# Products with the sines on GpSimd, and a sign moved to a later copy, in a two-branch sequence mixer

## The chip, the cores and the metric

The kernel runs on one core of one Trainium2 chip. The metric is the device time of one execution in microseconds (us), the median of three runs. A core has five engines that work side by side, each through its own queue in order: TensorE (PE, matmuls into PSUM; PEld is its weight load), VectorE (DVE), ScalarE (ACT), GpSimd (POOL) and SyncE (SP, which only issues DMAs here; ACT and POOL issue some too). They wait for each other by semaphores.

## The reference

Two branches read the same input of 2048 positions by 640 channels, and a gate by position mixes them:

```python
g = _sigmoid((x * gate_w).sum(-1, keepdims=True))
a = _A_ref(x, ...)      # long convolution by FFT with K, plus x * D_skip
b = _B_ref(x, ...)      # 2-D FFT, times a complex filter, inverse 2-D FFT
return g * a + (1 - g) * b
```

The convolution's kernel K is made from 128 complex modes for each of the 640 channels. This is the part that the change edits:

```python
dt = jnp.exp(log_dt)
A = -jnp.exp(log_A_real) + 1j * A_imag
C = (C_real + 1j * C_imag) * dt[:, None]
P = jnp.exp((A * dt[:, None])[:, :, None] * pos[None, None, :])
K = 2.0 * jnp.einsum("dn,dnl->dl", C, P).real
```

## The kernel before

**Phase P** turns the parameters into per-mode magnitudes and angles, `par`, in split high and low parts. **Phase A** transforms the input along the sequence: a first stage of small matmuls (`stage1`, L328), a copy out of PSUM, a second stage (`stage2`, L340), and the result goes to DRAM as `u_d`. The second half of the same function is the other branch: for each of nine groups of frequencies it loads `ue`, folds it (`fo`, `fg`), transposes it, transforms it along the channels (`p_d`), multiplies by the filter (`filt`, L528: `mm`, `zz`, `pm`), and transforms it back (`p_eo`, `p_i`). **Phase C** makes the first stage of K's transform, **phase D** the rest: the product of the two spectra, the inverse transform, the gates and the output.

**Phase B** makes K. It runs over 40 tiles of 16 channels each. K at position 64m + a is a product of two factors by mode: `y` for the 32 steps m and `x` for the 64 positions a, so that a matmul over the 128 modes (on the partitions) gives it. The positions a are counted from their middle, so that the two halves of 32 share the cosine and the sine of one angle: on the far half the angle has the other sign. One tile `t` has these steps:

- `mags` (L632): three matmuls `p_e` of 128x512 and three ACT exponentials give `e`, 16 channels by 96: 64 magnitudes for `x`, 32 for `y`. They run for five tiles (BT) in a row, so that ACT changes its table of functions twice for five tiles.
- `phases` (L643): two matmuls `p_p` give the angles in turns, ACT adds a large constant (L651) and DVE takes it away with the angle (L652), which leaves the reduced angle `q`, 1024 elements: the first 512 for `x`, the second for `y`.
- `trig` (L655): DVE clears the sign (`aq`, L662), and ACT makes four sines of 512 elements: the sines of `q` (sine) and of `aq` with a bias (cosine). For `y` they go to SBUF (`sc`, L665 and L666), for `x` to PSUM (`sx` L667, `cx` L668). `sx` and `cx` have one PSUM buffer each; `q`, `aq` and `sc` share five SBUF buffers.
- `prods` (L670): DVE multiplies the magnitudes by `sx` and `cx` (`x`, L675 to L677) and POOL by `sc` (`y`, L679 and L680).
- `kgen` (L682): 32 pairs of small matmuls of `y` and `x` accumulate `p_k` in PSUM, ACT copies two tiles at once to `kt` (L701), and every ten tiles go to DRAM as `k_d`.

`run` (L705) writes the order within phase B: in a burst of five tiles it takes `phases` and `trig` of tile t, then `prods` of t - 1, then a `kgen` some two tiles behind; between bursts come the five `mags`, with the `kgen` that are left. `merge` (L163) deals out the two streams, phase B against phases A and C, by the costs that each step yields (L228). Within that, a scheduler sets the final order of each engine's queue.

In phases C and D, `first` (L752) takes K's first transform: `stage1` with the table `e1` multiplies `kt`, and `S.copy` takes 512 columns at a time out of PSUM into `t1` (L336). What it copies has the 64 positions a of the real part on partitions 0 to 63, those of the imaginary part on 64 to 127, and in each the near half first.

## Time and profile before

| | |
|---|---|
| median of three runs | 609.23 us (608.76 to 611.23) |
| profiled execution | 608.74 us, of which the span of its instructions is 607.0 us |
| granted TensorE clock | 0.966 of full speed, mean |
| HBM | 60.91 MB read, 39.98 MB written, 166 GB/s over the span |

Three stages follow from the lines that run in them: up to 60 us the loads, phase P and the begin of phase A; from 60 to 430 us phase B beside the rest of phase A and the first of phase C; from 430 to 607 us phase D. The first sine of phase B stands at 72 us, its last product at 431 us.

A row of the groups of lines reads: line, engine, operation, what it writes <- what it reads, partitions x elements, count | busy us, mean ns of one | idle us of the engine before them, and what ended most of it. A row of waits reads: who, its line <- whom it waited for: us in total, times, longest. A row of the timeline: start us, duration us, engine, line, operation, operands.

### The profile page before, as it was taken

To read this page: it belongs to the slowest core of one execution; us is meant where nothing else is said; L and a number is where in the kernel's file an instruction comes from. 1 tells how busy PE (TensorE), PEld (TensorE's weight loads), DVE (VectorE), ACT (ScalarE), POOL (GpSimd) and SP (SyncE) were. 2 spreads that over 40 slices of the span, in tenths; PEclk is the share of its full clock that TensorE was granted. 3 is DMA by queue.
4 is the path that set the end of the run, shared out by engine and by line. 5 is a ranking of instruction groups with operands and counts; after the bars stand their busy time and mean duration, and the time that the engine had idled before them with its cause. 6 is when DMAs were issued, how large, how long until landed. Compare 5 with 4: busy or idle time off the path is not lost.

```text
span 607.0 us, 16654 instructions
## 1 busy us (share of the span) xinstructions
PE 535.8 (88%) x7084; PEld 405.6 (67%) x7084; DVE 500.2 (82%) x748; ACT 364.8 (60%) x659; POOL 267.0 (44%) x246
## 2 busy tenths in 40 slices
PE   9688979989968989989798999898989999999874
PEld 7576657766656657676566676565878877787631
DVE  5971597598899989999999899979399796987974
ACT  4556775576846876888589888799723332231210
POOL 4931252053525344454326335416254347547441
PEclk9899989989989996998899999999999999999998
DMA  8787204245612320332250233006685989889776
GB/s 341 293 288 268 79 5 151 69 154 181 239 43 67 97 87 13 108 118 109 67 151 12 75 97 110 24 28 200 224 346 184 356 273 299 291 271 310 225 231 239
DMA packets 48083, 101.98 MB, mean 168 GB/s; under 512 B 3316, under 2 KB 32776, under 8 KB 46248
## 3 DMA queue, kind: packets, MB, share of 16 engines
q1 hardware_dynamic: 24888, 67.74, 32.3%
q10 hardware_dynamic: 20080, 22.52, 11.9%
q0 software_dynamic: 3040, 10.65, 5.3%
q8 instruction: 56, 0.92, 0.6%
q14 instruction: 19, 0.16, 0.1%
HBM read 60.91 MB, written 39.98 MB: 166 GB/s over the span
## 4 chain that ended last, share of the span: by engine, by line
PE 51%; DVE 27%; ACT 9%; DMA 8%; issue 4%; POOL 1%; ACTq 0%; DVEq 0%; POOLq 0%; SPq 0%
PE p_eo L551 8%; PE p_s L348 8%; PE p_s L335 6%; PE p_e L638 5%; PE p_k L693 4%; PE p_i L814 4%; PE p_p L649 3%; DVE q L652 3%; PE p_d L518 2%; DVE t L801 2%; PE p_i L565 2%; PE p_t L502 2%; DVE ma L795 2%; PE p_c L893 2%; PE p_d L519 2%
## 5 line engine op out<-in xcount | busy, mean ns | idle before, releaser
L679 POOL TENSOR_TENSOR y<-e,sc 128x512 f32<-128x512 f32 x40 | 56.7, 1418 | 131.0 <-ACT sc L665 60.3
L348 PE MATMUL p_s<-t,w 128*64 128x160 f32 x1056 | 92.4, 314 | 10.2 <-ACT ut L382 5.1
L348 PEld LDWEIGHTS p_s<-t,w 128*64 128x64 f32 x1056 | 76.5, 139 | 21.4 <-ACT ut L382 6.0
L640 ACT ACTIVATE e<-p_e 128x512 f32<-128x512 f32 x120 | 68.6, 602 | 22.7 <-PE p_e L638 20.4
L551 PE MATMUL p_eo<-td,pmt 107*128 107x321 f32 x204 | 69.0, 459 | 3.9 <-ACT pmt L505 3.9
L693 PE MATMUL p_k<-x,y 128*32 128x64 f32 x2560 | 63.6, 229 | 9.8 <-DVE x L677 2.9
L693 PEld LDWEIGHTS p_k<-x,y 128*32 128x32 f32 x2560 | 46.1, 113 | 38.0 <-issue 29.4
L652 DVE SCALAR_TENSOR_TENSOR q<-q,p_p 128x512 f32<-128x512 f32 x80 | 53.4, 681 | 13.5 <-ACT q L651 11.8
L336 ACT COPY t<-p_s 128x512 f32<-128x512 f32 x40 | 24.6, 623 | 65.2 <-PE p_s L335 41.8
L638 PE MATMUL p_e<-rm,par 128*128 128x512 f32 x120 | 58.7, 519 | 3.4 <-ACT e L640 2.8
L680 POOL TENSOR_TENSOR y<-e,sc 128x512 f32<-128x512 f32 x40 | 54.5, 1362 | 6.5 <-ACT sc L666 6.5
L800 POOL TENSOR_TENSOR t<-ma 64x320 f32<-64x320 f32 x32 | 28.0, 875 | 61.4 <-DVE ma L795 51.8
L551 PEld LDWEIGHTS p_eo<-td,pmt 107*128 107x128 f32 x204 | 38.4, 198 | 19.6 <-ACT pmt L505 6.9
L677 DVE TENSOR_TENSOR x<-e,cx 128x1024 f32<-128x1024 f32 x40 | 48.6, 1214 | 2.2 <-ACT cx L668 2.2
L651 ACT ACTIVATE q<-p_p 128x512 f32<-128x512 f32 x80 | 46.5, 592 | 4.2 <-PE p_p L649 3.8
L649 PE MATMUL p_p<-rp,par 128*128 128x512 f32 x80 | 43.5, 548 | 4.5 <-DVE q L652 4.5
L814 PE MATMUL p_i<-t,w 128*64 128x160 f32 x528 | 42.7, 300 | 4.4 <-POOL t L801 3.4
L335 PE MATMUL p_s<-c,kt 128*64 128x128 f32 x640 | 43.0, 274 | 3.9 <-DVE mb L796 2.0
L335 PEld LDWEIGHTS p_s<-c,kt 128*64 128x64 f32 x640 | 38.0, 136 | 12.6 <-issue 7.7
L816 ACT COPY s<-p_i 128x640 f32<-128x640 f32 x32 | 21.8, 694 | 40.0 <-PE p_i L814 30.4
L335 PE MATMUL p_s<-c,u 128*64 128x128 f32 x640 | 41.5, 278 | 2.5 <-ACT ut L382 2.5
L795 DVE TENSOR_TENSOR ma<-p_s,us 128x640 f32<-128x640 f32 (+1 forms) x36 | 28.2, 784 | 18.8 <-PE p_s L348 11.5
(153 smaller groups left out, 1181.5 us busy)
## 6 DMA issues: line engine op xcount, KB each, us to landing
u_d<-ut SPq DMA_DIRECT2D x32, 320.0 KB, 2.6
us<-u_d ACTq DMA_DIRECT2D x16, 640.0 KB, 6.0
s_d<-s ACTq DMA_DIRECT2D x15, 640.0 KB, 8.3
t<-s_d SPq DMA_DIRECT2D x14, 640.0 KB, 5.9
ww<-in_w_l SPq DMA_DIRECT2D x8, 642.0 KB, 4.0
ue<-u_d SPq DMA_DIRECT2D x8, 640.0 KB, 4.4
k_d<-kt SPq DMA_DIRECT2D x4, 1280.0 KB, 7.6
kt<-k_d SPq DMA_DIRECT2D x8, 640.0 KB, 5.9
```

What stands on the lines that cost most here:

```text
L335: nc.tensor.matmul(p[64 * ri:64 * ri + 64, j, :], src(i + j), e1[ri], start=True, stop=True)
L348: ins = nc.tensor.matmul(p[64 * j:64 * j + 64, i, 160 * ri:160 * ri + 160], w2[:, x, 64 * ri:64 * ri + 64], t1[:, x // 2 if x < 32 else K0 ...
L551: P.matmul(p[:, :E], st.pmt[:DC, c, w, j, :], tv[:DC, w, c, :], start=c == 0, stop=c == 2)
L638: P.matmul(p[:, :], pars[t], rm[:, c:c + 512], start=True, stop=True)
L640: st.exp = S.activation(ef[:, c:c + 512], p[:, :], AF.Exp)
L649: P.matmul(p[:, :], pars[t], rp[:, c:c + 512], start=True, stop=True)
L652: V.scalar_tensor_tensor(out=qf[:, c:c + 512], in0=qf[:, c:c + 512], scalar=MAGIC, in1=p[:, :], op0=ALU.subtract, op1=ALU.subtract)
L677: V.tensor_tensor(out=x[:, 0].rearrange("p d (h j) -> p d h j", h=2), in0=e[:, :, 0:64].rearrange("p d (h j) -> p d h j", h=2), in1=cx.uns ...
L679: G.tensor_tensor(out=y[:, 1], in0=e[:, :, 64:96], in1=sc[:, 0], op=ALU.mult)
L680: G.tensor_tensor(out=y[:, 0], in0=e[:, :, 64:96], in1=sc[:, 1], op=ALU.mult)
L693: P.matmul(st.pb[32 * r:32 * r + 32, o, :], y[:, ri, 4 * qq + JR[r], :], x[:, ri, 4 * qq + JR[r], :], start=t % 2 + qq + 1 - ri == 0, stop ...
L814: T.mm = P.matmul(p[x:x + 64, i // 2, 160 * (i % 2):160 * (i % 2) + 160], T.w3[:, k0 + h + i, x:x + 64], t2[:, h + i, :], start=True, stop ...
```

## The change

ACT writes the sines over `q` and the `y` half of the cosines over `aq`, in SBUF; only `cx` stays in PSUM, with two buffers in place of one each for `cx` and `sx`. POOL makes the products with `sx`, both halves in one operation of 1024 elements with the sine broadcast over the two halves, between its two products of `y`. DVE makes the products with `cx`, one half plain and the far half times -1. Before, the far half's sine product carried the -1; now its cosine product does, so that the far half of `x` has the opposite sign as a whole. That sign goes through `kgen`, `k_d` and `stage1`, and is taken away where `first` copies out of PSUM: `near` scales each partition by +1 or -1 from a new column of the constant table. The skip term of `kgen` is untouched.

```diff
+        np.tile(np.repeat([1.0, -1.0], 32), 2)[:, None], np.full((128, 1), HALF_PI)], 1)
...
+        T.sa = take(1)
...
-    pt = ctx.enter_context(tc.tile_pool(name="b_pt", reuse_waits="tile", bufs=1, space=PSUM))
+    pt = ctx.enter_context(tc.tile_pool(name="b_pt", reuse_waits="tile", bufs=2, space=PSUM))
...
     def trig(t, r):
-        aq = wt.tile([128, 2, 16, 32], F32, tag="w", name="aq")
-        sc = r.sc = wt.tile([128, 2, 16, 32], F32, tag="w", name="sc")
-        sx, cx = r.sx, r.cx = [pt.tile([128, 16, 32], F32, tag=n, name=n) for n in ("sx", "cx")]
+        aq = r.aq = wt.tile([128, 2, 16, 32], F32, tag="w", name="aq")
+        cx = r.cx = pt.tile([128, 16, 32], F32, tag="cx", name="cx")
...
-            S.activation(fl(sc[:, 0]), r.q[:, 512:1024], AF.Sin, scale=TWO_PI)
-        S.activation(fl(sc[:, 1]), af[:, 512:1024], AF.Sin, scale=-TWO_PI, bias=T.hpi)
-        S.activation(fl(sx), r.q[:, 0:512], AF.Sin, scale=TWO_PI)
-        T.trig = st.trig = S.activation(fl(cx), af[:, 0:512], AF.Sin, scale=-TWO_PI, bias=T.hpi)
+            S.activation(r.q[:, 512:1024], r.q[:, 512:1024], AF.Sin, scale=TWO_PI)
+        S.activation(r.q[:, 0:512], r.q[:, 0:512], AF.Sin, scale=TWO_PI)
+        S.activation(fl(cx), af[:, 0:512], AF.Sin, scale=-TWO_PI, bias=T.hpi)
+        T.trig = st.trig = S.activation(af[:, 512:1024], af[:, 512:1024], AF.Sin, scale=-TWO_PI, bias=T.hpi)
...
     def prods(t, r):
-        V.scalar_tensor_tensor(out=x[:, 1, :, 32:64], in0=e[:, :, 32:64], scalar=-1.0, in1=sx[:, :, :], op0=ALU.mult, op1=ALU.mult)
-        V.tensor_tensor(out=x[:, 1, :, 0:32], in0=e[:, :, 0:32], in1=sx[:, :, :], op=ALU.mult)
-        V.tensor_tensor(out=x[:, 0].rearrange("p d (h j) -> p d h j", h=2), in0=e[:, :, 0:64].rearrange("p d (h j) -> p d h j", h=2),
-                        in1=cx.unsqueeze(2).broadcast_to([128, 16, 2, 32]), op=ALU.mult)
-        G.tensor_tensor(out=y[:, 1], in0=e[:, :, 64:96], in1=sc[:, 0], op=ALU.mult)
-        G.tensor_tensor(out=y[:, 0], in0=e[:, :, 64:96], in1=sc[:, 1], op=ALU.mult)
+        V.tensor_tensor(out=x[:, 0, :, 0:32], in0=e[:, :, 0:32], in1=cx[:, :, :], op=ALU.mult)
+        V.scalar_tensor_tensor(out=x[:, 0, :, 32:64], in0=e[:, :, 32:64], scalar=-1.0, in1=cx[:, :, :], op0=ALU.mult, op1=ALU.mult)
+        G.tensor_tensor(out=y[:, 1], in0=e[:, :, 64:96], in1=si[:, 1], op=ALU.mult)
+        G.tensor_tensor(out=x[:, 1].rearrange("p d (h j) -> p d h j", h=2), in0=e[:, :, 0:64].rearrange("p d (h j) -> p d h j", h=2),
+                        in1=si[:, 0].unsqueeze(2).broadcast_to([128, 16, 2, 32]), op=ALU.mult)
+        G.tensor_tensor(out=y[:, 0], in0=e[:, :, 64:96], in1=r.aq[:, 1], op=ALU.mult)
...
+    def near(dst, src):
+        S.activation(dst, src, AF.Copy, scale=T.sa)
...
-            yield from stage1(nc, ps, T.e1, lambda q: T.kt[c, h][:, q, :], 20, t1v[:, 80 * h:80 * h + 80], S.copy)
+            yield from stage1(nc, ps, T.e1, lambda q: T.kt[c, h][:, q, :], 20, t1v[:, 80 * h:80 * h + 80], near)
```

`si` is `q` seen as two halves of 16 channels by 32. Line numbers after the change are one higher than before from the constant table's slices on, and five higher behind `near`; in `trig` and `prods` the sines stand on L664 to L667, DVE's products on L676 and L677, POOL's on L678, L679 and L681.

The change moves instructions on every queue of phase B. POOL's queue, at the first tiles of phase B, before:

```order
L679 TENSOR_TENSOR y<-e,sc 128x512
L680 TENSOR_TENSOR y<-e,sc 128x512
L679 TENSOR_TENSOR y<-e,sc 128x512
L680 TENSOR_TENSOR y<-e,sc 128x512
L679 TENSOR_TENSOR y<-e,sc 128x512
L394 TENSOR_TENSOR z<-c_65,gw 128x640
L680 TENSOR_TENSOR y<-e,sc 128x512
L628 DMA par<-par_d 128x640
```

and the same place after:

```order
L678 TENSOR_TENSOR y<-e,q 128x512
L679 TENSOR_TENSOR x<-e,q 128x1024
L681 TENSOR_TENSOR y<-e,aq 128x512
L678 TENSOR_TENSOR y<-e,q 128x512
L679 TENSOR_TENSOR x<-e,q 128x1024
L681 TENSOR_TENSOR y<-e,aq 128x512
L395 TENSOR_TENSOR z<-c_65,gw 128x640
L678 TENSOR_TENSOR y<-e,q 128x512
L679 TENSOR_TENSOR x<-e,q 128x1024
L629 DMA par<-par_d 128x640
```

Three products a tile stand where two stood, the long one between the two of `y`. ACT's queue in the second half of the second burst, before (the copies of `q` are L651, the sines L665 to L668):

```order
L667 ACTIVATE sx<-q 128x512
L665 ACTIVATE sc<-q 128x512
L651 ACTIVATE q<-p_p 128x512
L666 ACTIVATE sc<-aq,c_65 128x512
L668 ACTIVATE cx<-aq,c_65 128x512
L651 ACTIVATE q<-p_p 128x512
L667 ACTIVATE sx<-q 128x512
L420 COPY lg<-p_g 128x64
L701 COPY kt<-p_k 128x512
L665 ACTIVATE sc<-q 128x512
L651 ACTIVATE q<-p_p 128x512
L666 ACTIVATE sc<-aq,c_65 128x512
```

and after:

```order
L652 ACTIVATE q<-p_p 128x512 x2
L421 COPY lg<-p_g 128x64
L652 ACTIVATE q<-p_p 128x512 x2
L664 ACTIVATE q<-q 128x512
L665 ACTIVATE q<-q 128x512
L666 ACTIVATE cx<-aq,c_65 128x512
L667 ACTIVATE aq<-aq,c_65 128x512
L664 ACTIVATE q<-q 128x512
L665 ACTIVATE q<-q 128x512
L666 ACTIVATE cx<-aq,c_65 128x512
L667 ACTIVATE aq<-aq,c_65 128x512
```

The sines of a tile now stand together, and the copies of `q` of later tiles ahead of them, where the two were interleaved. PE's queue around the first products of phase B (`p_k`), before (`p_p` are the angles' matmuls, two a tile; `p_s` and `p_g` belong to phase A):

```order
L649 MATMUL p_p<-rp,par 128x512
L417 MATMUL p_g<-u,z 32x64 x10
L335 MATMUL p_s_947<-c_65,u 64x128 x5
L649 MATMUL p_p<-rp,par 128x512
L335 MATMUL p_s_947<-c_65,u 64x128 x3
L335 MATMUL p_s_982<-c_65,u 64x128 x8
L335 MATMUL p_s_1013<-c_65,u 64x128 x8
L693 MATMUL p_k<-x,y 32x64 x4
```

and after:

```order
L650 MATMUL p_p<-rp,par 128x512
L336 MATMUL p_s_945<-c_65,u 64x128 x3
L336 MATMUL p_s_978<-c_65,u 64x128 x7
L650 MATMUL p_p<-rp,par 128x512
L336 MATMUL p_s_978<-c_65,u 64x128
L336 MATMUL p_s_1007<-c_65,u 64x128 x3
L650 MATMUL p_p<-rp,par 128x512
L336 MATMUL p_s_1007<-c_65,u 64x128 x5
L336 MATMUL p_s_1069<-c_65,u 64x128 x8
L336 MATMUL p_s_1079<-c_65,u 64x128 x5
L694 MATMUL p_k<-x,y 32x64 x4
```

Four `p_p` stand ahead of the first `p_k` before, six after: the angles of one more tile.

More of the change, by code (lines that the diff above doesn't have):

```diff
@@ L76, in _tables @@
         np.repeat([-1.0, 1.0], 64)[:, None], np.repeat([1.0, -1.0], 64)[:, None],
-        np.full((128, 1), HALF_PI)], 1)
+        np.tile(np.repeat([1.0, -1.0], 32), 2)[:, None], np.full((128, 1), HALF_PI)], 1)
     k = np.array(POS_K)
```

3 lines of the change are left out of this document (2 added, 1 removed).

## The prediction

> **What bounds the kernel now.** I read the page's busy times and chain first, then the span cut into stages, then the groups of lines in the middle stage, and last the rows of VectorE (DVE) and GpSimd (POOL) side by side.
>
> ```profile
> PE 535.8 (88%) x7084; PEld 405.6 (67%) x7084; DVE 500.2 (82%) x748; ACT 364.8 (60%) x659; POOL 267.0 (44%) x246
> ...
> PE 51%; DVE 27%; ACT 9%; DMA 8%; issue 4%; POOL 1%; ACTq 0%; DVEq 0%; POOLq 0%; SPq 0%
> ```
>
> The second row is the chain of waits, shares of 607.0 us. Then the stage from 60 to 430 us:
>
> ```profile
> core 0: us, PE busy (x) PEld busy (x) DVE busy (x) ACT busy (x) POOL busy (x), PEclk, DMA share, GB/s
> ...
> 60.00:430.00 370.00, 334.97 (x4419) 244.21 (x4415) 327.55 (x498) 283.56 (x519) 153.94 (x129) 0.95 0.30 95
> ```
>
> This is where phase B (the tiles that the change edits) runs merged with phases A and C. There PE is busy 335 of 370 us and DVE 328, so both are nearly full and PE has 35 us of idle time. POOL has 216 us free. So the change takes work from an engine that counts and gives it to one that seems to have room. In the last stage (phase D) only the copy of `near` is touched.
>
> **What is taken off DVE and put on POOL.**
>
> ```profile
> L679 POOL TENSOR_TENSOR y<-e,sc 128x512 f32<-128x512 f32 x40 | 56.7, 1418 | 131.0 <-ACT sc L665 60.3 <-issue 58.8 <-DVE qq L557 11.7
> L680 POOL TENSOR_TENSOR y<-e,sc 128x512 f32<-128x512 f32 x40 | 54.5, 1362 | 6.5 <-ACT sc L666 6.5
> ...
> L677 DVE TENSOR_TENSOR x<-e,cx 128x1024 f32<-128x1024 f32 x40 | 48.6, 1214 | 2.2 <-ACT cx L668 2.2
> ...
> L676 DVE TENSOR_TENSOR x<-e,sx 128x512 f32<-128x512 f32 x40 | 27.2, 679 | 0.0
> L675 DVE SCALAR_TENSOR_TENSOR x<-e,sx 128x512 f32<-128x512 f32 x40 | 27.2, 679 | 0.6 <-ACT sx L667 0.6
> ...
> L487 POOL TENSOR_TENSOR fg<-fo 128x318 f32<-128x318 f32 x8 | 15.2, 1896 | 35.7 <-DVE fo L481 25.2 <-PE p_t L502 6.7 <-PE p_d L519 3.9
> ...
> L394 POOL TENSOR_TENSOR z<-c,gw 128x640 f32<-128x640 f32 x8 | 10.6, 1336 | 28.1 <-PE p_g L417 21.4 <-DMA gw<-in_gw_l 6.8
> ...
> L486 POOL TENSOR_TENSOR fg<-fo 128x318 f32<-128x318 f32 x8 | 10.3, 1292 | 2.4 <-DVE fo L482 2.4
> ```
>
> Before, DVE makes three products a tile: two of 512 elements with the sine (679 ns each) and one of 1024 with the cosine (1214 ns). After, it makes two of 512 with the cosine, one of them with the -1, read from PSUM as before. So 40 x 1214 ns = **48.6 us** leave DVE, 15% of what it does in the middle stage.
>
> POOL gets 40 products of 128x1024. No such operation of POOL is in the trace. By the 128x640 product, 1336 ns x 1024/640 = 2.1 us; by the 128x512 one, 2 x 1418 = 2.8 us. The inner rows of 32 elements are those of `y`, so I take 2.7 us: 40 x 2.7 = **107 us**, and POOL's 154 us in the stage become about 261 of 370. POOL does not run out of time on average.
>
> **What the two engines do to each other.**
>
> ```profile
> 202.38 0.49 DVE L535 TENSOR_TENSOR zz<-mm 128x321 f32<-128x321 f32 x1
> ...
> 288.50 1.29 POOL L679 TENSOR_TENSOR y<-e,sc 128x512 f32<-128x512 f32 x1
> ...
> 289.29 2.41 DVE L536 TENSOR_TENSOR mm<-xx,ww 128x642 f32<-128x642 f32 x1
> ...
> 289.74 1.26 POOL L680 TENSOR_TENSOR y<-e,sc 128x512 f32<-128x512 f32 x1
> ...
> 291.62 0.68 DVE L652 SCALAR_TENSOR_TENSOR q<-q,p_p 128x512 f32<-128x512 f32 x1
> ...
> 292.22 0.81 DVE L537 TENSOR_TENSOR mm<-xx,ww 128x642 f32<-128x642 f32 x1
> ...
> 292.96 0.68 DVE L662 TENSOR_SCALAR aq<-q 128x1024 int32<-128x1024 int32 x1
> ...
> 295.05 1.55 DVE L539 TENSOR_TENSOR zz<-mm 128x321 f32<-128x321 f32 x1
> ```
>
> L537, with no POOL operation beside it, takes 0.81 us. Its twin L536 starts while POOL makes a `y`, POOL begins the next at 289.74, and L536 ends 0.70 us after that one (291.00): it stood still for two POOL operations. L539 takes 1.55 us in the same way, three times the 0.49 of such an operation alone (first row). DVE operations with SBUF operands alone do this; those that read PSUM (L675 to L677, 679, 679 and 1214 ns on average) don't. The groups that suffer:
>
> ```profile
> L662 DVE TENSOR_SCALAR aq<-q 128x1024 int32<-128x1024 int32 x40 | 30.7, 767 | 0.2
> ...
> L482 DVE TENSOR_TENSOR fo<-ue 128x640 f32<-128x640 f32 x8 | 8.8, 1095 | 0.0
> L536 DVE TENSOR_TENSOR mm<-xx,ww 128x642 f32<-128x642 f32 x8 | 8.3, 1036 | 0.0
> ...
> L541 DVE TENSOR_TENSOR pm<-zz 128x642 f32<-128x642 f32 x8 | 7.7, 960 | 0.0
> L533 DVE TENSOR_TENSOR mm<-xx,ww 128x642 f32<-128x642 f32 x8 | 7.6, 954 | 0.0
> L487 DVE TENSOR_TENSOR fg<-fo 128x318 f32<-128x318 f32 x8 | 7.6, 945 | 0.0
> ...
> L486 DVE TENSOR_TENSOR fg<-fo 128x318 f32<-128x318 f32 x8 | 7.4, 926 | 0.0
> ...
> L542 DVE TENSOR_TENSOR pm<-zz 128x642 f32<-128x642 f32 x8 | 7.3, 906 | 0.0
> L532 DVE TENSOR_TENSOR mm<-xx,ww 128x642 f32<-128x642 f32 x8 | 7.2, 905 | 0.0
> ...
> L538 DVE TENSOR_TENSOR zz<-mm 128x321 f32<-128x321 f32 x8 | 6.1, 761 | 0.0
> L539 DVE TENSOR_TENSOR zz<-mm 128x321 f32<-128x321 f32 x8 | 6.0, 752 | 0.0
> ...
> L535 DVE TENSOR_TENSOR zz<-mm 128x321 f32<-128x321 f32 x8 | 4.6, 578 | 0.0
> ...
> L534 DVE TENSOR_TENSOR zz<-mm 128x321 f32<-128x321 f32 x8 | 4.2, 523 | 0.8 <-PE p_t L502 0.7
> ```
>
> Undisturbed they would be 40 x 0.68 (L662), 48 x 0.82 (the wide `fo`, `mm` and `pm`) and 48 x 0.49 us (`zz` and `fg`) = 27.2 + 39.4 + 23.5 = 90 us; they sum to 113.5. So DVE loses **23 us** now to POOL's products, which run for 56.7 + 54.5 + 15.2 + 10.3 = 137 us, 37% of the stage.
>
> After, they run for 137 + 107 = 244 us, 66%. A DVE operation that meets one waits on average for half of it: 0.7 us for those of today, 1.35 for the new ones. The loss goes with occupancy times length: 23 x (137 x 0.7 + 107 x 1.35) / (137 x 0.7) = 58 us, **35 more**. Bounds: 0 if the new products happened to fall where DVE works on PSUM; 23 x 107/137 = 18 by occupancy alone; and if 66% of these 136 operations waited the full half length, 0.98 us on average, 88 us, so 65 more. (The same count for today gives 136 x 37% x 0.7 = 35, where 23 are seen, so the upper end is far.) I take 35. DVE's 48.6 us shrink to 14.
>
> [...]
>
> **What of it lies on the path.** DVE is 27% of the chain, 164 us, of 500 busy: so of each microsecond of DVE work a third lies on the path.
>
> ```profile
> by line: PE p_eo L551 12.7%; PE p_e L638 8.1%; PE p_k L693 6.8%; PE p_s L348 5.2%; PE p_p L649 4.2%; DVE q L652 4.1%; PE p_s L335 4.0%; PE p_d L518 4.0%; PE p_i L565 3.7%; PE p_t L502 3.5%; PE p_d L519 3.4%; DVE x L677 2.8%; issue 2.8%; DVE
> ```
>
> (The chain of waits from 60 to 430 us by line.) L677, the product whose length goes, is 2.8% of 370 us: **-10.4 us**. At a third, the 35 us of added waits are **+12 us**; ends 0 and 65/3 = +22.
>
> **Waits that move.**
>
> ```profile
> ACT sx L667 <- DVE x L676: 5.3, 4, 4.6
> ...
> PEld p_k L693 <- POOL y L680: 3.7, 4, 2.1
> ...
> PEld p_k L693 <- POOL y L679: 2.4, 4, 0.8
> ...
> PE p_k L693 <- POOL y L680: 2.0, 1, 2.0
> ```
>
> PE waits for POOL's last product 9 times, 8.1 us. That product now comes 2.7 us later in each tile. Against it, PE's order puts the first products `p_k` two `p_p` later than before (the rows above). Ends: 0, and 9 x 2.7 = 24 us; I take that the waits grow by half, **+4 us**. Behind a waiting `p_k` all of PE's other work is queued, phase A's and C's too. The `par` loads on POOL's queue are issued a batch of five tiles ahead, some 45 us, and stay hidden.
>
> The in-place sines wait for DVE's `aq` (L662), which reads the same `q`; two of four sines didn't. That is up to 40 x 0.68 = 27 us of ACT waiting, covered by the next tile's copies of `q`, which stand ahead of the sines in ACT's new order; ACT is 9% of 607 us of chain in 365 busy, 15%, so between 0 and +4: **+2 us**. Without that cover it is the 4. The second buffer of `cx` and the absent `sx` take away the 5.3 us of the first row: at 15%, **-1 us**, at most -5.
>
> ```profile
> L336 ACT COPY t<-p_s 128x512 f32<-128x512 f32 x40 | 24.6, 623 | 65.2 <-PE p_s L335 41.8 <-PE p_i L814 10.3 <-DVE mb L796 7.7
> ...
> L505 ACT ACTIVATE pmt<-p_t,td 107x512 f32<-107x512 f32 x24 | 15.8, 698 | 4.4 <-PE p_t L502 4.4
> ```
>
> `near` is a scaled ACTIVATE in place of a COPY: 40 x (698 - 623) = 3 us, in groups before which ACT idles 65 us: **0**. If PE waited for each, 3.
>
> **The sum**, on the profiled execution (608.74 us, span 607.0; the median of the three runs, 609.23, is 0.5 above): 608.7 - 10.4 + 12 + 4 + 2 - 1 = **615.3**, so 615.
>
> **The rivals.** *DVE's relief comes through* (faster). For it: L677's own share of the chain, and 216 us of free time on POOL. The new products need only fall beside DVE's PSUM work, and the double `cx` lets ACT run ahead. Then the waits grow by 18 us at most, +6 on the path, and PE waits stay: 608.7 - 16 (a third of 48.6) + 6 = 599. Against it: L536's 2.41 us, and PE's 90% in the stage.
>
> *They cancel*: DVE's 14 us net count a third, 5, and the late products and the sines' wait cost as much: 608.7 - 5 + 5 = 609.
>
> *POOL sets the pace* (much slower). In a burst of five tiles POOL needs 1.3 + 2.7 + 1.3 us a tile and lets DVE's 0.68 us `aq` in between, 6.0 us, or 30 a burst; DVE needs 2 x 0.68 (L652) + 0.68 (L662) + 2.57 = 4.6 us a tile today. `q` and `aq` live in five buffers, freed now by POOL, two tiles behind. From the point where POOL is over two tiles behind, `aq` waits in DVE's queue with everything behind it. If half of the 8 x 5 x 1.4 us shows: +28, 637. Against it: the magnitudes that follow each burst give POOL time to catch up.
>
> **How the numbers follow.** Forecast, 612 to 626 by the bounds of the terms taken one at a time, chance 0.40; relief 0.32; cancel 0.20; pace 0.08. A measurement here tells about 0.5% (3 us) from no change: faster 0.32, same 0.20, slower 0.48. The range must reach into the relief case, so 599; its upper end holds either unknown most of the way to its bound (waits +22 in place of +12 gives 625, late `p_k` +24 in place of +4 gives 635): 630.
>
> **What would show it.** In the new profile: POOL near 375 us; L679 near 2.7 us; the means of L536 to L542 (one line down) well above 1 us; DVE near 487 us, not 452; more of PE waiting for POOL's `x` and `y`. If the SBUF groups of DVE stay at today's means, the step of the waits is wrong, and the time is near 599.

## The result, and the profile after

| | before | after |
|---|---|---|
| median, six runs each on the same chip | 609.00 us (606.77 to 614.64) | 665.95 us (664.06 to 670.01) |
| ratio | | **1.0935**, 95% interval 1.0876 to 1.0994 |
| profiled execution, its span | 608.74, 607.0 us | 666.69, 664.9 us |
| granted TensorE clock, mean | 0.966 | 0.914 |

The kernel became 9.4% slower. The prediction, 615 us, had the direction; the time lies 36 us above the upper end of its range. A ratio here and below compares only executions in the faster of the two states that they fall into, so it can differ a little from the quotient of two medians.

The page of the changed kernel, busy times of the engines:

```profile
PE 561.8 (84%) x7084; PEld 422.0 (63%) x7084; DVE 508.2 (76%) x708; ACT 369.1 (56%) x659; POOL 356.2 (54%) x286
```

and the span cut into stages; phase B now ends at about 490 us instead of 430:

```profile
core 0: us, PE busy (x) PEld busy (x) DVE busy (x) ACT busy (x) POOL busy (x), PEclk, DMA share, GB/s
...
60.00:490.00 430.00, 361.24 (x4469) 261.05 (x4468) 336.92 (x460) 286.75 (x523) 243.55 (x169) 0.88 0.26 82
490.00:665.00 175.00, 152.41 (x1890) 119.62 (x1888) 135.10 (x199) 49.83 (x76) 83.78 (x90) 0.99 0.83 279
```

The last stage takes 175 us, 177 before: all of the loss lies in the middle stage, which is 60 us longer. Two columns divide these 60. PE's busy time there went from 334.97 to 361.24 us, 26.3 more. In the whole span it is 26.0 more (561.8 against 535.8) for the same 7084 matmuls: they ran slower, in this stage at a mean granted clock of 0.88 instead of 0.95. The other 33.7 us are PE's idle time, 35.0 before and 68.8 now.

The groups of lines of the changed kernel:

```profile
L678 POOL TENSOR_TENSOR y<-e,q 128x512 f32<-128x512 f32 x40 | 52.0, 1301 | 128.3 <-ACT q L664 90.4
...
L679 POOL TENSOR_TENSOR x<-e,q 128x1024 f32<-128x1024 f32 x40 | 100.9, 2522 | 0.0
...
L694 PE MATMUL p_k<-x,y 128*32 128x64 f32 x2560 | 67.2, 237 | 31.7 <-POOL x L679 21.1
L552 PE MATMUL p_eo<-td,pmt 107*128 107x321 f32 x204 | 80.9, 518 | 12.6 <-ACT pmt L506 12.6
...
L755 ACT ACTIVATE t<-p_s,c 128x512 f32<-128x512 f32 x40 | 28.6, 721 | 64.9 <-PE p_s L336 41.8
...
L681 POOL TENSOR_TENSOR y<-e,aq 128x512 f32<-128x512 f32 x40 | 60.2, 1506 | 0.1
...
L662 DVE TENSOR_SCALAR aq<-q 128x1024 int32<-128x1024 int32 x40 | 56.1, 1403 | 0.6
```

POOL's new product takes 2.52 us, and POOL is not full: it is busy 244 of 430 us. `aq` (L662) takes 1403 ns on average, 767 before, and DVE hardly idles ahead of it (0.6 us in all): it does not wait for a buffer, it stands while it runs. The matmul `p_eo` (L552), which the change doesn't touch, takes 518 ns instead of 459: that is the clock. Those of its 204 matmuls that ran wholly at half clock, 46 here and 8 before, took 0.76 us on average, those at full clock 0.44.

The rows of DVE and POOL side by side show how DVE stands (start us, duration us; a bracket is the idle time ahead):

```profile
265.49 5.74 DVE L533 TENSOR_TENSOR mm<-xx,ww 128x642 f32<-128x642 f32 x1
...
265.70 1.31 POOL L678 TENSOR_TENSOR y<-e,q 128x512 f32<-128x512 f32 x1
...
266.95 2.37 POOL L679 TENSOR_TENSOR x<-e,q 128x1024 f32<-128x1024 f32 x1
...
269.27 1.27 POOL L681 TENSOR_TENSOR y<-e,aq 128x512 f32<-128x512 f32 x1
271.15 0.68 DVE L662 TENSOR_SCALAR aq<-q 128x1024 int32<-128x1024 int32 x1
...
271.87 0.63 ACT L664 ACTIVATE q<-q 128x512 f32<-128x512 f32 x1 [4.11 <-DVE aq L662]
```

L533, 0.81 us at its shortest, took 5.74 us. It began just ahead of POOL's three products, while POOL issued a `par` load, and ended only 0.69 us after the last of them: here DVE did not get in between the products, though POOL changed instructions twice. `aq` stood behind it in DVE's queue, so ACT waited 4.11 us with its sines and with all copies out of PSUM queued behind them.

This is the longest case, and not the rule. A usual one:

```profile
215.91 2.94 POOL L679 TENSOR_TENSOR x<-e,q 128x1024 f32<-128x1024 f32 x1
216.56 2.97 DVE L534 TENSOR_TENSOR mm<-xx,ww 128x642 f32<-128x642 f32 x1
218.82 1.85 POOL L681 TENSOR_TENSOR y<-e,aq 128x512 f32<-128x512 f32 x1
```

L534 ends at 219.53, 0.68 us after L679 and inside L681, which took 1.85 us where its shortest takes 1.25: DVE ran when POOL passed to its next product, and that product stood. In the records from 60 us to POOL's last `y`, 47 of DVE's instructions that took over 0.15 us above their shortest were held while one POOL instruction gave way to the next within 0.1 us. 42 of them ran at the first such change; five were passed over. These five stood 17 us, of 72.6 us that DVE's instructions stood in all.

The waits that end late, over the whole span (us, times, longest):

```profile
ACT q L664 <- DVE aq L662: 38.8, 17, 5.6
...
PEld p_k L694 <- POOL x L679: 24.2, 12, 5.6
PE p_k L694 <- POOL x L679: 21.1, 10, 5.4
...
PEld p_k L694 <- POOL y L681: 10.4, 8, 2.3
PE p_k L694 <- POOL y L681: 8.3, 6, 2.1
```

ACT's waits for `aq` were 7.5 us before. PE's for POOL's products, 8.1 us in the rows of before, sum to 64.0 in the same two columns (PE's own are 29.4 of them).

And this is how a wait costs PE twice. The span of the changed kernel in pieces of 3.41 us, around one wait for POOL's `x`:

```profile
core 0: us, PE busy (x) PEld busy (x) DVE busy (x) ACT busy (x) POOL busy (x), PEclk, DMA share, GB/s
...
239.95:243.36 3.41, 3.41 (x62) 2.52 (x60) 3.41 (x7) 3.13 (x5) 0.00 (x0) 1.00 0.17 71
243.36:246.77 3.41, 0.21 (x2) 0.00 (x0) 3.41 (x4) 2.20 (x5) 3.41 (x3) 1.00 0.00 0
246.77:250.18 3.41, 0.44 (x8) 0.20 (x8) 3.41 (x4) 3.41 (x7) 3.41 (x3) 0.50 0.01 2
250.18:253.60 3.42, 2.11 (x65) 2.09 (x66) 1.91 (x4) 1.08 (x3) 3.42 (x4) 0.50 0.02 5
253.60:257.01 3.41, 3.41 (x14) 3.31 (x14) 1.73 (x1) 0.57 (x2) 2.87 (x3) 0.50 0.00 0
257.01:260.43 3.42, 3.42 (x24) 3.13 (x23) 3.42 (x7) 2.42 (x6) 0.61 (x1) 1.00 0.21 28
```

In the second piece PE is busy 0.21 us, still at clock 1.00; the three pieces behind it run at 0.50, the last of them with PE busy throughout, and only then is the clock back at 1.00. Cut in this way at the clock's own edges, the records of this run hold 160 pieces at full clock with a piece behind them. In the 20 that are followed by half clock PE was busy at most 65% of the time; of the other 140, nine were below that. At half clock PE spent 114 us of the span, 41 before.

The levels in this trace are 1.00 and 0.50, and each stretch at one level, but the last, lasted a whole number of pieces of 3.41 us. Pieces with PE busy as much as 0.65 of the time were followed by half clock, so pauses that add up to a third of a piece came before some of the drops. Not every such piece was followed by one: of the 29 at full clock in which PE was busy 0.65 of the time or less, 20 were.

### The profile page after: what moved, and what is told of

It is laid out like the page before. It is cut to its first block, busy times and chain, and to the rows that moved or that the text cites. A ratio compares the mean times of both kernels' runs of the same rounds, so it can differ in the third digit from the quotient of the medians.

```text
span 664.9 us, 16708 instructions
## 1 busy us (share of the span) xinstructions
PE 561.8 (84%) x7084; PEld 422.0 (63%) x7084; DVE 508.2 (76%) x708; ACT 369.1 (56%) x659; POOL 356.2 (54%) x286
## 5 line engine op out<-in xcount | busy, mean ns | idle before, releaser
L678 POOL TENSOR_TENSOR y<-e,q 128x512 f32<-128x512 f32 x40 | 52.0, 1301 | 128.3 <-ACT q L664 90.4
L349 PE MATMUL p_s<-t,w 128*64 128x160 f32 x1056 | 97.4, 320 | 13.7 <-ACT ut L383 5.1
L679 POOL TENSOR_TENSOR x<-e,q 128x1024 f32<-128x1024 f32 x40 | 100.9, 2522 | 0.0
L694 PE MATMUL p_k<-x,y 128*32 128x64 f32 x2560 | 67.2, 237 | 31.7 <-POOL x L679 21.1
L552 PE MATMUL p_eo<-td,pmt 107*128 107x321 f32 x204 | 80.9, 518 | 12.6 <-ACT pmt L506 12.6
L653 DVE SCALAR_TENSOR_TENSOR q<-q,p_p 128x512 f32<-128x512 f32 x80 | 53.1, 681 | 22.4 <-ACT q L652 20.5
L639 PE MATMUL p_e<-rm,par 128*128 128x512 f32 x120 | 62.9, 552 | 8.5 <-ACT e L641 5.4
L755 ACT ACTIVATE t<-p_s,c 128x512 f32<-128x512 f32 x40 | 28.6, 721 | 64.9 <-PE p_s L336 41.8
L552 PEld LDWEIGHTS p_eo<-td,pmt 107*128 107x128 f32 x204 | 44.3, 227 | 30.4 <-ACT pmt L506 14.8
L681 POOL TENSOR_TENSOR y<-e,aq 128x512 f32<-128x512 f32 x40 | 60.2, 1506 | 0.1
L662 DVE TENSOR_SCALAR aq<-q 128x1024 int32<-128x1024 int32 x40 | 56.1, 1403 | 0.6
L664 ACT ACTIVATE q<-q 128x512 f32<-128x512 f32 x40 | 25.1, 628 | 39.0 <-DVE aq L662 38.8
```

The costliest lines, as they stand in the source:

```text
L349: ins = nc.tensor.matmul(p[64 * j:64 * j + 64, i, 160 * ri:160 * ri + 160], w2[:, x, 64 * ri:64 * ri + 64], t1[:, x // 2 if x < 32 else K0 ...
L552: P.matmul(p[:, :E], st.pmt[:DC, c, w, j, :], tv[:DC, w, c, :], start=c == 0, stop=c == 2)
L639: P.matmul(p[:, :], pars[t], rm[:, c:c + 512], start=True, stop=True)
L653: V.scalar_tensor_tensor(out=qf[:, c:c + 512], in0=qf[:, c:c + 512], scalar=MAGIC, in1=p[:, :], op0=ALU.subtract, op1=ALU.subtract)
L662: V.tensor_scalar(out=af.bitcast(I32), in0=r.q.bitcast(I32), scalar1=0x7FFFFFFF, scalar2=None, op0=ALU.bitwise_and)
L678: G.tensor_tensor(out=y[:, 1], in0=e[:, :, 64:96], in1=si[:, 1], op=ALU.mult)
```

## The experiments

The loss could come from four places: DVE's relief that brings nothing, DVE standing behind POOL, POOL's product arriving late at PE, or the new arrangement of the sines. All ratios are to the kernel before, measured beside it on the same chip.

### The small parts: the copy `near`, the sign, and y's sines in place

**near_only** is the kernel before with the scaled copy in place of the plain one (scale 1):

```diff
+    def near(dst, src):
+        S.activation(dst, src, AF.Copy, scale=T.sa)
...
-  ..., t1v[:, 80 * h:80 * h + 80], S.copy)
+  ..., t1v[:, 80 * h:80 * h + 80], near)
```

> The kernel of before with only the copy of K's first transform made a scaled ACTIVATE, the scale all ones. If the scaled copy is what costs 1% with the sign moved, 613 to 616 us; if it is the order of DVE's products, 609.

Measured: 612.0 us, ratio 1.0064 (1.0022 to 1.0106).

**sign_only** adds the sign: DVE makes all three products from PSUM as before, but the cosine product is the one in two halves with the -1.

```diff
-        V...(out=x[:, 1, :, 32:64], in0=e[:, :, 32:64], scalar=-1.0, in1=sx ...)
-        V...(out=x[:, 1, :, 0:32], in0=e[:, :, 0:32], in1=sx ...)
-        V...(out=x[:, 0] ..., in0=e[:, :, 0:64] ..., in1=cx.unsqueeze(2) ...)
+        V...(out=x[:, 1] ..., in0=e[:, :, 0:64] ..., in1=sx.unsqueeze(2) ...)
+        V...(out=x[:, 0, :, 0:32], in0=e[:, :, 0:32], in1=cx ...)
+        V...(out=x[:, 0, :, 32:64], in0=e[:, :, 32:64], scalar=-1.0, in1=cx ...)
```

> The kernel of before with the sign alone moved: DVE still makes all four products from PSUM (the sine in one operation of 1024, the cosine in two of 512), and the copy of K's first transform is the scaled one. Theory L (DVE's SBUF operations stand still behind POOL's longer run of products) and theory P (POOL hands its product over too late, PE waits): both say no change, 609 us within 0.5%, POOL at 267 us busy. If the sign or the scaled copy cost something, 615 or more.

Measured: 614.63 us, ratio 1.0097 (1.0055 to 1.0140).

**inplace_y** is sign_only with `y`'s sines written over `q` and `aq` as in the changed kernel; `x`'s stay in PSUM and on DVE.

```diff
-            S.activation(fl(sc[:, 0]), r.q[:, 512:1024], AF.Sin, scale=TWO_PI)
-        S.activation(fl(sc[:, 1]), af[:, 512:1024], AF.Sin, scale=-TWO_PI, bias=T.hpi)
+            S.activation(r.q[:, 512:1024], r.q[:, 512:1024], AF.Sin, scale=TWO_PI)
+        S.activation(af[:, 512:1024], af[:, 512:1024], AF.Sin, scale=-TWO_PI, bias=T.hpi)
```

> The kernel of before with the sign moved and the two sines for y written over q and aq; the sines for x stay in PSUM and DVE makes all four products from there, POOL only the two of y. What it adds to the sign alone (614.6 us) is that the first sine for y must wait for DVE's aq. If the in-place sines alone explain the 5% of the version with DVE's product from SBUF, 630 to 640 us; if that was DVE's two-input SBUF products (69 us busy against 48.6), 612 to 620.

Measured: 608.70 us, ratio 1.0060 (1.0015 to 1.0105). The three intervals overlap, so the scaled copy is all that can be seen: about 4 us, by the middle of near_only's ratio. The sign and `y`'s sines in place add nothing that shows beside it.

### What DVE's relief is worth

**drop_x** is the changed kernel without POOL's sine product, and PE doesn't wait for it.

```diff
-        x = wk.tile([128, 2, 16, 64], F32, tag="x", name="x")
+        x = wk.tile([128, 1, 16, 64], F32, tag="x", name="x")
-        G.tensor_tensor(out=x[:, 1] ..., in0=e[:, :, 0:64] ..., in1=si[:, 0] ..., op=ALU.mult)
-   ... y[:, ri, 4 * qq + JR[r], :], x[:, ri, 4 * qq + JR[r], :],
+   ... y[:, ri, 4 * qq + JR[r], :], x[:, 0, 4 * qq + JR[r], :],
```

> The changed kernel without the sine product: nobody makes it, the matmuls take the cosine product for both parts. POOL has its two products of y as before, DVE is 48.6 us lighter, and ACT's sines stand four in a row as with the change. This is what the relief of DVE is worth if POOL cost nothing: L and P both say 585 to 605 us, half-clock time of PE 35 us or less. If the new order of ACT's queue is a loss of its own, 610 to 630.

Measured: 618.23 us, ratio 1.0186 (1.0119 to 1.0253). With all of the relief and nothing of POOL's product it is still slower than before. **before_drop** takes the same kind of relief in the old order: the kernel before without its two products with `sx`.

```diff
-        V.scalar_tensor_tensor(out=x[:, 1, :, 32:64], in0=e[:, :, 32:64], scalar=-1.0, in1=sx ...)
-        V.tensor_tensor(out=x[:, 1, :, 0:32], in0=e[:, :, 0:32], in1=sx ...)
-   ... x[:, ri, 4 * qq + JR[r], :],
+   ... x[:, 0, 4 * qq + JR[r], :],
```

> The kernel before without its two products with sx (40 x 2 x 0.68 = 54 us off DVE); ACT still makes sx, nobody reads it, and the matmuls read the cosine product twice: the sine part of K is left out. Nothing else moves: sines, their buffers, near and POOL's queue are those of before. Theory 'DVE's work is not what sets the stage': within 1% of before (603 to 615 us), as drop_x found no gain either. Rival 'the relief is worth a third of its length, as the chain says, and the in-place sines of drop_x ate it': -11 to -18 us, ratio 0.97 to 0.98.

Measured: 607.19 us (12 runs), ratio 1.0028 (0.9992 to 1.0063). The stage of its profile:

```profile
60.00:430.00 370.00, 337.65 (x4539) 249.06 (x4539) 291.25 (x418) 287.34 (x528) 147.97 (x129) 0.95 0.30 96
```

DVE is busy 291 us where it was 328, and PE's busy time and clock stay (338 and 0.95, before 335 and 0.95). So 54 us less work for DVE bought nothing that shows: the amount of DVE's work did not set the length of the stage, whatever its share of the chain.

**drop_cx1** asks whether drop_x is slow because its four sines stand in a row in ACT's queue. Its `x` sine goes to PSUM again, unread, with one buffer of `cx`; ACT's queue then mixes sines and copies as before.

```diff
-    pt = ...(name="b_pt", reuse_waits="tile", bufs=2, space=PSUM)
+    pt = ...(name="b_pt", reuse_waits="tile", bufs=1, space=PSUM)
...
+        sx = pt.tile([128, 16, 32], F32, tag="sx", name="sx")
-        S.activation(r.q[:, 0:512], r.q[:, 0:512], AF.Sin, scale=TWO_PI)
+        S.activation(fl(sx), r.q[:, 0:512], AF.Sin, scale=TWO_PI)
```

> drop_x with the x sine in PSUM again (sx, unread, one buffer) and one buffer of cx instead of two; the other two sines stay in place and near stays. The sine part of K is left out as in drop_x. ACT's queue then mixes the sines with the copies out of PSUM again, where drop_x has four sines in a row. Theory 'the bunch of four sines ahead of ACT's copies is what made drop_x 1.9% slower than before': ratio near that of before_drop, 0.98 to 1.005. Rival 'the in-place sines or near did it': ratio near drop_x, 1.015 to 1.02. If the scatter of such orders is itself 1 to 2%, neither will be seen.

Measured: 615.29 us, ratio 1.0147 (1.0095 to 1.0199). It overlaps drop_x: the bunch of sines was not shown to be the cause. The step from before_drop to drop_x, 1.0028 to 1.0186 or some 10 us, holds the 4 us of `near`; the rest belongs to the new arrangement as a whole and was not taken apart. It does not show as more idle time of PE (33.8 us in drop_x's stage, 34.7 before) but as more time at half clock (64.9 us, 34.1 before).

### What POOL's products do to DVE

**lock_only** is inplace_y with two more products of 128x512 on POOL per tile, behind those of `y`, whose result nobody reads. DVE keeps all its work.

```diff
+        for h in (0, 32):
+            with after(g0):
+                g0 = G.tensor_tensor(out=si[:, 0], in0=e[:, :, h:h + 32], in1=r.aq[:, 1], op=ALU.mult)
```

> The kernel with the sign moved and y's sines in place (608.7 us), in which DVE still makes all products from PSUM; POOL makes two more products of 512 elements a tile, behind its two of y, into the spent first half of q, which nothing reads. So POOL has 40 x 2.6 us more and reads SBUF for as long as in the changed kernel, but PE waits for none of it and nothing is taken off DVE. L: DVE's excess rises from 25 to 65 us or more, and the time to 640 to 680 us. If POOL's reading hurts only because the product is late for PE: 605 to 615.

Measured: 639.23 us, ratio 1.0463 (1.0367 to 1.0560), against inplace_y's 1.0060: 4.0% for POOL's added work, with nothing taken off DVE. Its group of `aq`, and one stretch of its timeline:

```profile
L663 DVE TENSOR_SCALAR aq<-q 128x1024 int32<-128x1024 int32 x40 | 49.1, 1228 | 0.3
```

```profile
307.84 1.27 POOL L681 TENSOR_TENSOR y<-e,q 128x512 f32<-128x512 f32 x1
307.94 4.31 DVE L537 TENSOR_TENSOR mm<-xx,ww 128x642 f32<-128x642 f32 x1
309.06 1.26 POOL L682 TENSOR_TENSOR y<-e,aq 128x512 f32<-128x512 f32 x1
310.29 3.09 POOL L685 TENSOR_TENSOR q<-e,aq 128x512 f32<-128x512 f32 x2
```

DVE's L537 stands behind three products of POOL. The last row groups two; `mm` ends at 312.25, inside that row, so it ran ahead of the second of them, which POOL began 0.08 us after the first. Some of PE's waits for POOL grew here too (PE's own from 4.8 us in inplace_y's stage to 9.7), since the next tile's `y` comes later, so not all of the 4.0% need be DVE's.

**idle_write** is drop_x with three memsets a tile on POOL, into a tile that nobody reads, last in each tile: 3 x 992 ns, about the time of the product (2522), but POOL only writes.

```diff
-        G.tensor_tensor(out=y[:, 0], in0=e[:, :, 64:96], in1=r.aq[:, 1], op=ALU.mult)
+        g1 = G.tensor_tensor(out=y[:, 0], in0=e[:, :, 64:96], in1=r.aq[:, 1], op=ALU.mult)
+        for _ in range(3):
+            with after(g1):
+                g1 = G.memset(xd[:, :, :], 0.5)
```

> As the version in which POOL only writes constants, but into a tile that nothing reads and behind both products of y, so that PE doesn't wait for it either. Both losses are out, the stand of two-input operations and the late product; what is left against the version without any sine product is what writes of POOL do to DVE (aq above all). L and P together: 590 to 615 us; if aq's stand behind POOL's writes is the larger part, 625 to 645.

Measured: 632.91 us, ratio 1.0426 (1.0374 to 1.0479), above drop_x. A stretch of its timeline:

```profile
351.51 4.22 DVE L662 TENSOR_SCALAR aq<-q 128x1024 int32<-128x1024 int32 x1
351.79 1.28 POOL L679 TENSOR_TENSOR y<-e,q 128x512 f32<-128x512 f32 x1
353.02 1.28 POOL L680 TENSOR_TENSOR y<-e,aq 128x512 f32<-128x512 f32 x1
354.23 3.41 POOL L683 MEMSET xd<- 128x1024 f32 x3
...
356.57 0.83 DVE L537 TENSOR_TENSOR mm<-xx,ww 128x642 f32<-128x642 f32 x1
```

`aq`, with one input, stands over both products and a memset and ends at 355.73; `mm` (L537), two inputs from SBUF, runs beside the third in its ordinary 0.83 us. Over the stage it is the same: of DVE's `mm`, `pm` and `zz`, 21 met memsets alone (an overlap of under 0.1 us with anything else left aside) and took at most 0.83 us (wide) and 0.48 us (narrow); seven `aq` met memsets alone and took 1.25 us on average, against 0.69 for those that met nothing. So in this run POOL's memsets held up `aq` and not `mm`, `pm` and `zz`. They differ in more than the number of inputs (`aq` is a TENSOR_SCALAR on int32, the others are TENSOR_TENSOR on f32), and no run takes that apart.

**dead_x** has POOL's real product instead of the memsets, again last in the tile and read by nobody.

```diff
+        with after(g0):
+            G.tensor_tensor(out=xd ..., in0=e[:, :, 0:64] ..., in1=si[:, 0] ..., op=ALU.mult)
```

> POOL makes its two products of y first and then the product with the sine into a tile that nothing reads; the matmuls take the cosine product for both parts, so the sine's part of K is left out. POOL's and DVE's work and their use of SBUF are those of the changed kernel, but PE never waits for POOL's long product. L: still slow, 645 to 670 us, mean of L662 above 1.2 us. P: the waits of p_k for POOL fall to those of before, and the time to 605 to 615 us.

Measured: 660.23 us, ratio 1.0822 (1.0727 to 1.0916). Of the changed kernel's 9.4%, 8.2 are there with a product for which PE hardly ever waits (0.4 us). In the stage, PE's own waits for POOL fall from 29.4 us in the changed kernel to 7.2, and those for DVE rise from 15.1 to 34.8 (before: 2.1 and 17.8): with the late product gone, PE waits for DVE instead. Against idle_write, the product in place of the memsets adds 4.0%: now the two-input instructions stand longer as well (mean of `mm` L538 1.61 us against 1.13 there, of `fo` L483 1.54 against 0.82).

**halves** makes POOL's product in two operations of 512, to let DVE in between. The program has the second behind `y`'s last; in the order that ran, it stands right behind the first in all 40 tiles (`y`, `x`, `x`, `y`), so it is the long product cut in two in its place.

```diff
+        G.tensor_tensor(out=x[:, 1, :, 0:32], in0=e[:, :, 0:32], in1=si[:, 0], op=ALU.mult)
...
+        G.tensor_tensor(out=x[:, 1, :, 32:64], in0=e[:, :, 32:64], in1=si[:, 0], op=ALU.mult)
```

> The changed kernel with POOL's long product cut into two of 512 elements, the second behind the last y. POOL works as long in all (4 x 1.3 us a tile). Theory L, if DVE gets in between any two of POOL's operations: no single stand over 1.4 us, and 630 to 650 us. If POOL's operations in a row keep DVE out as one would: stands of 4 to 5 us as with the changed kernel, and 655 to 675.

Measured: 670.88 us, ratio 1.1094 (1.1008 to 1.1179). Shorter operations do not help. The time lies where the expectation put a run that keeps DVE out as one, and the longest stand is still 5.0 us. But the trace does not bear out that reason: of 52 DVE instructions held at a change from one POOL instruction to the next, 48 ran at the first change, and in all DVE stood 66.5 us, less than the changed kernel's 72.6. PE still waits for POOL's `x` (26.1 us of PEld, 23.7 of PE) and spends more time at half clock (119.5 us against 102.4). Why halves is the slower of the two stays open.

**abs_act** takes `aq` off DVE and gives it to ACT.

```diff
-        V.tensor_scalar(out=af.bitcast(I32), in0=r.q.bitcast(I32), scalar1=0x7FFFFFFF, ...)
+        S.activation(af, r.q, AF.Abs)
```

> The changed kernel with the absolute value aq made by ACT (one operation of 1024, an estimated 1.1 us, 40 of them) instead of DVE, so that the chain q, aq, sine no longer goes through DVE's queue and DVE's aq can't stand behind POOL. POOL's product stays. If aq's waits (56 us busy against 31, and 39 us of ACT waiting for it) are the main loss, 615 to 635 us; if the other DVE operations that stand behind POOL, or PE's waits for POOL's product, are, 645 to 670.

Measured: 677.78 us, ratio 1.1190 (1.1115 to 1.1265). One row of its groups:

```profile
L662 ACT ACTIVATE aq<-q 128x1024 f32<-128x1024 f32 x40 | 42.3, 1058 | 51.1 <-DVE q L653 51.1
```

ACT now has 42 us more, and waits 51 us for DVE's `q` (L653), which stands in DVE's queue behind other instructions that POOL holds up (once behind an `fg`, L487, of 5.73 us). So `aq` is only one of the places where DVE stands; taking it away moved ACT's wait by one instruction. The time lies above both ranges of the expectation. DVE stands 17 us less than in the changed kernel, but PE's waits for POOL's `x` grew from 24.2 and 21.1 us to 41.1 (PEld) and 36.8 (PE): what is saved in one queue came back in another.

**one_in_five** lets POOL make the sine product for the last tile of each burst alone, and DVE from PSUM for the other four.

```diff
+        if r.far:
+            G.tensor_tensor(out=x[:, 1] ..., in1=si[:, 0] ..., op=ALU.mult)
+        else:
+            V.tensor_tensor(out=x[:, 1] ..., in1=r.sx ..., op=ALU.mult)
```

> The changed kernel with POOL making the sine product for the last tile of each burst alone (8 of 40); the other 32 have the sine in PSUM and their product on DVE, one buffer each for cx and sx. If the loss goes with POOL's added time, a fifth of 57 us: 615 to 625. If a single long run of POOL's products a burst is hidden in the exponentials that follow, and DVE's relief counts, 600 to 610.

Measured: 620.27 us, ratio 1.0213 (1.0135 to 1.0290). Neither share of the sine product on POOL, 40 tiles or 8, beats the kernel before.

### The late product

**no_read** puts three memsets into `x` itself in the place of the product, so that PE waits for them as it waits for the product.

```diff
+        for _ in range(3):
+            with after(g1):
+                g1 = G.memset(x[:, 1], 0.5)
```

> POOL writes constants into the sine's half of x, three times in a row, in place of the product (the sine's part of K is left out). PE waits for it as it does for the product, and POOL is busy for about as long (1 us or less for each of the three, not seen before), but it reads nothing from SBUF. L: DVE operations with two SBUF inputs go free, the means of L533 to L543 fall to those of before or lower, and the time to 600 to 620 us; what is left above 609 is what aq (one input, int32) still loses. P: as slow as the changed kernel, 645 to 670 us, if POOL is busy for 340 us or more.

Measured: 647.90 us, ratio 1.0617 (1.0513 to 1.0722). Its waits:

```profile
PEld p_k L696 <- POOL x L681: 20.2, 11, 4.9
...
PE p_k L696 <- POOL x L681: 17.3, 7, 4.7
```

Against idle_write, where POOL does the same work but PE does not wait for it, that is 1.9% or 12 us. With the real product (dead_x against the changed kernel) the step is 1.1%, and those intervals overlap.

**inplace_dve** is the changed kernel with the sine product on DVE, still from SBUF.

```diff
-        G.tensor_tensor(out=x[:, 1] ..., in1=si[:, 0] ..., op=ALU.mult)
+        V.tensor_tensor(out=x[:, 1] ..., in1=si[:, 0] ..., op=ALU.mult)
```

> The changed kernel with the sine product made by DVE instead of POOL, all else as changed (sines in place, cx with two buffers, one order of sines, sign moved). DVE gets 40 operations of 128x1024 with two SBUF inputs, about 1.1 us each alone. L and P: the excess goes with POOL's 101 us, so 605 to 620 us, with POOL near 267 us busy, and the mean of L662 back under 0.85 us. A third theory O (the in-place sines that all wait for aq, or the new order of the queues) says it stays above 640.

Measured: 640.61 us, ratio 1.0499 (1.0397 to 1.0601). Its product among the groups:

```profile
L679 DVE TENSOR_TENSOR x<-e,q 128x1024 f32<-128x1024 f32 x40 | 69.0, 1725 | 3.5 <-ACT q L665 3.5
```

The same product from PSUM took 1214 ns; with both inputs in SBUF it takes 1725 on average (its shortest 1205, where the expectation had 1.1 us alone), as it now meets POOL's two products of `y` (1466 and 1647 ns, before 1418 and 1362). sign_only, where DVE makes the same products with sines from PSUM, stands at 1.0097, and drop_x, which has the same sines in SBUF and no sine product, at 1.0186. So the place of the sines is at most a part; some 3% more come when DVE makes the product from SBUF, for which PE now waits (21.6 us for this `x`). The time is at the edge of what the expectation gave to theory O (above 640), but drop_x, with O's sines and order, is far below it. L and P, which put it at 605 to 620 us, had left out this wait.

### The runs side by side

From the records of each profiled run, in the stage from 60 us to POOL's last `y`: how long DVE's instructions took above the shortest of their line and shape (summed, and the longest single one), PE's idle time (neither matmul nor weight load), and the time at half clock.

| kernel | ratio | DVE standing, us | longest | PE idle, us | half clock, us |
|---|---|---|---|---|---|
| before | 1 | 27.1 | 1.6 | 34.7 | 34.1 |
| before_drop | 1.0028 | 33.0 | 3.5 | 31.9 | 34.1 |
| inplace_y | 1.0060 | 25.5 | 1.1 | 33.5 | 34.1 |
| drop_x | 1.0186 | 29.5 | 1.1 | 33.8 | 64.9 |
| one_in_five | 1.0213 | 29.4 | 2.2 | 35.1 | 52.3 |
| idle_write | 1.0426 | 49.8 | 3.5 | 42.1 | 88.7 |
| lock_only | 1.0463 | 53.4 | 3.5 | 44.5 | 82.7 |
| inplace_dve | 1.0499 | 41.6 | 1.1 | 51.8 | 71.7 |
| no_read | 1.0617 | 47.2 | 2.2 | 56.7 | 95.6 |
| dead_x | 1.0822 | 73.5 | 5.5 | 60.6 | 94.7 |
| after | 1.0935 | 72.6 | 4.9 | 68.5 | 102.4 |
| halves | 1.1094 | 66.5 | 5.0 | 66.4 | 119.5 |
| abs_act | 1.1190 | 56.0 | 5.3 | 79.3 | 111.5 |

Taken in this order, the way from before to after goes, in per cent: relief and nothing else, 0; the new arrangement and `near`, 1.6; POOL's occupancy and its writes (three memsets a tile), 2.4; the product in their place, which also reads, 4.0; the product late for PE, 1.1 (not told from 0 there, 1.9 in no_read). These are differences between runs, each with the waits of PE and the half clock that came with it, and not separate prices. The last two rows, with less standing than the changed kernel and more time, show that DVE's standing does not set the time alone.

## Why the prediction was wrong

The step that failed most is the price of DVE's waits: charged +12 us, where the runs show up to 39 (the 2.4% and 4.0% above). Beside it, the relief was charged -10.4 and is worth 0, the late product +4 and costs 7 to 12, and the sines' place, the buffer of `cx` and `near` together +1 and cost some 10.

**DVE's relief, -10.4 us: wrong, 0.** The step took L677's share of the chain, 2.8% of the stage, as the price of its removal. before_drop removes 54 us of DVE's work and gains nothing. The chain lists what was last at each step. That other paths of nearly the same length stand beside it, in a stage where PE is busy nine tenths of the time, is a likely reason; no run shows it. The share was an upper bound.

**DVE's waits: the size was right, the price was wrong.** The forecast was a loss of 58 us in L662 and twelve groups of the other branch, 35 more than before. The same groups after, with shapes kept apart:

```profile
L662 DVE TENSOR_SCALAR aq<-q 128x1024 int32<-128x1024 int32 x40 | 56.1, 1403 | 0.6
L533 DVE TENSOR_TENSOR mm<-xx,ww 128x642 f32<-128x642 f32 x8 | 12.9, 1618 | 0.0
L534 DVE TENSOR_TENSOR mm<-xx,ww 128x642 f32<-128x642 f32 x8 | 11.7, 1459 | 0.0
...
L543 DVE TENSOR_TENSOR pm<-zz 128x642 f32<-128x642 f32 x8 | 10.5, 1308 | 0.0
...
L537 DVE TENSOR_TENSOR mm<-xx,ww 128x642 f32<-128x642 f32 x8 | 8.6, 1078 | 0.2
L542 DVE TENSOR_TENSOR pm<-zz 128x642 f32<-128x642 f32 x8 | 8.0, 1002 | 0.1
L488 DVE TENSOR_TENSOR fg<-fo 128x318 f32<-128x318 f32 x8 | 7.8, 977 | 0.0
L483 DVE TENSOR_TENSOR fo<-ue 128x640 f32<-128x640 f32 x8 | 7.2, 897 | 0.0
L487 DVE TENSOR_TENSOR fg<-fo 128x318 f32<-128x318 f32 x8 | 6.5, 809 | 1.4 <-PE p_t L503 1.4
L535 DVE TENSOR_TENSOR zz<-mm 128x321 f32<-128x321 f32 x8 | 6.3, 793 | 6.0 <-PE p_t L503 5.9
L540 DVE TENSOR_TENSOR zz<-mm 128x321 f32<-128x321 f32 x8 | 6.1, 766 | 0.0
L539 DVE TENSOR_TENSOR zz<-mm 128x321 f32<-128x321 f32 x8 | 5.2, 654 | 0.1
...
L536 DVE TENSOR_TENSOR zz<-mm 128x321 f32<-128x321 f32 x8 | 3.9, 482 | 0.0
```

They sum to 150.8 us; less the 90 undisturbed that is 61, 37 more than the 23.5 of before. Outside these groups L538, whose twin of before was not held up, stands some 4 us now, and over the stage DVE stands 45 us more than before (72.6 against 27.1). But the step then charged a third of it, +12, by DVE's share of the chain. The runs show about the whole: lock_only stands 28 us more than inplace_y and takes 4.0%, 24 us, more; idle_write 20 more than drop_x for 2.4%, 15 us; dead_x 24 more than idle_write for 4.0%, 24 us. These prices include what POOL's later products did to PE, so they are upper ends, and no fixed rate: halves and abs_act stand less than the changed kernel and take longer. Why a microsecond of standing costs so much more than a third is not shown by a run of its own. What the traces show is who waits: ACT 4.11 us for one `aq` above, and PE 34.8 us for DVE in dead_x, 17.8 before. To count with half of one POOL product, as the prediction did, was right in sum. The row that it started from, L536 standing for two in a row, is the exception in its own trace: of 20 DVE instructions held at such a change there, 19 ran at the first.

**Late `x` and `y`, +4 with a bound of 24: too small.** The rows that summed to 8.1 us sum to 64.0. What it cost by itself is 7 us (dead_x to after, not told from 0) to 12 us (idle_write to no_read). The rest overlaps waits that are there without it: PE is idle 60.6 us in dead_x, where it doesn't wait for the product, and 68.5 after.

**Sines in place +2, `cx` -1, `near` 0.** `near` costs about 4 us (1.0064), above the 3 that the text gave as its bound, though the interval (1.3 to 6.4 us) holds the 3; that ACT idles ahead of these copies did not hide it. `y`'s sines in place show nothing. The arrangement as a whole, with `x`'s sine, brings some 6 us more (before_drop to drop_x, less `near`), where the sum had +1.

**Left out: the clock.** No term of the sum spoke of the granted clock, though the column stood in the quoted row of the stage (0.95). PE's same matmuls took 26 us more, nearly half of the 60. The differences between the runs above contain what half clock adds; it does not come on top of them.

**The rivals.** The relief that comes through is refuted by before_drop, and that the two cancel by the time. The pace case, 637 us, was nearest in time, but it named a wait of `aq` for buffers behind POOL, and DVE's 0.6 us of idle time ahead of L662 shows none. Of the signs that the text listed, POOL was to be near 375 us (356), L679 near 2.7 (2.52), the means of L537 to L543 well above 1 us (in part: 1.0 to 1.3 for the wide ones, 0.65 and 0.77 for the narrow), DVE 487 (508), and more of PE waiting for POOL (yes). So DVE's standing and PE's waits for POOL were named ahead and priced too low; the clock, and most of what the new arrangement costs, were not named.

## What to carry to other kernels

Work moved from VectorE to GpSimd was paid for here where VectorE's SBUF instructions stood (72.6 us in the stage, 27.1 before), not where GpSimd ran out of time (busy 244 of 430 us). Look at the longest run of GpSimd instructions in a row, and see who is queued behind a VectorE instruction that stands for all of it: here L533 took 5.74 us behind three products, and ACT waited 4.11 us for the `aq` behind it. That was the worst case; in 42 of 47 the wait was only for the rest of one GpSimd instruction. A share of the chain of waits bounded the gain from above here and did not give the price of a delay; try the removal alone before moving anything. Where PE is busy nine tenths of a stage, as in this one before the change, count its waits with the half clock that may follow them: 114 us of this span ran at half clock, 41 before.

## What the runs showed of the hardware

- A DVE instruction held by GpSimd ran, in 42 of 47 cases of the changed kernel, when GpSimd passed to its next instruction; in the case shown, that one then stood (L681 1.85 us behind L534, 1.25 at its shortest). Five times it was passed over, at worst 5.74 us behind three products.
- In idle_write, GpSimd's memsets alone held up DVE's one-input `aq` (1.25 us on average beside them, 0.69 for those that met nothing), but not the two-input `mm`, `pm` and `zz` (at most 0.83 and 0.48 us).
- PE's clock went between 1.00 and 0.50 in pieces of 3.41 us, and of the 29 such pieces of the changed kernel at full clock with PE busy 0.65 or less, 20 were followed by half clock.
